# Attention with a top-32 search, a dense layer and a routed layer: which engine copies the last 64 keys of each tile into the search's tile

## The chip, the cores and the metric

The kernel runs on one core of a Trainium2 chip. The time is device time in microseconds (us) of one execution. Engines are called TensorE (PE; PEld is its weight load), VectorE (DVE), ScalarE (ACT), GpSimd (POOL) and SyncE (SP), as the profile's rows call them in brackets.

## What is computed

Three stages, one after the other, in float32:

```python
# q, k, v: (4, 8, 576, 64)
scores = np.matmul(q, k.transpose(0, 1, 3, 2)) / np.sqrt(64)
kth = np.partition(scores, -32, axis=-1)[..., -32:-31]
scores = np.where(scores >= kth, scores, -1e9)
attn = softmax(scores); x = attn @ v                 # then (2304, 512)
h = x @ w_in                                         # 512 -> 2048
x = (np.maximum(h, 0) + np.log1p(np.exp(-np.abs(h)))) @ w_out
# routed layer: 8 experts, each token goes to the argmax of x @ w_gate
out[mask] = gate[mask] * (np.maximum(x[mask] @ w1[e], 0) @ w2[e])
```

For every query row the 32nd largest of its 576 scores has to be found. That search is what the change touches.

## The kernel before

*Part one* computes attention and the dense layers, *part two* the routed layer. A tile is 128 query rows of one head; two tiles make a group, and there are 72 groups. Ten units of one or two finished row blocks go through the dense layers; a unit starts when the products of its last group are done. A unit has 16 steps: 12 matmuls into a bank (L646), two ScalarE functions (L660, L661) and the second layer's matmuls (L686).

For a group `emit_scores` has TensorE write the scores of the first 256 keys into bank `sa`, which ScalarE copies to the tile `s` (L466), and those of the other 320 keys into the tile `sb` in PSUM, one bank for each of its two tiles (L456). There is one buffer of `sa` and one of `sb`. `emit_softmax` then searches:

- L496 to L499 on VectorE take the larger of two keys, then of four, for the first 512 keys. L496 writes into a free part of `sb`, L497 into `s`, L498 and L499 into the tile `wk`: the larger halves in columns 0 to 127, the smaller in 128 to 255.
- L500 copies the last 64 keys of both tiles from `sb` into columns 256 to 319 of `wk`.
- L501 on VectorE writes the smaller ones of the first pairing into the last 256 columns of `wk`.
- L502 on ScalarE copies the 320 scores from `sb` to `s`. After it TensorE may write the next group's scores into `sb`.
- L506, L518 and L522 on VectorE find eight maxima at a time, four times, and strike them out between. The first two rounds look at 128 columns, the third at 320, the fourth at all 576.
- L529 on ScalarE scales the 32nd value; L530 (ScalarE), L531 (GpSimd), L532 (ScalarE, the exponential), L540 (ScalarE) and L541, L542 (GpSimd) make the weights, which a DMA transposes. The products with v (L559, L561) follow three groups later, and L583 to L586 on VectorE scale them.

In the first groups VectorE (L249, L252), ScalarE (L247, L251, L258, L259) and GpSimd also decode the dense layers' weights.

The program is written group by group, but the order on each engine is set by a scheduler, which sorts the instructions with priorities given in the code and a model of their times. A change of one instruction moves others. Engines run their own instructions in order and wait for each other by semaphores.

Of the kernel before, what the change touches and what calls it, by code (L numbers as in the profile page):

```python
# [13 lines left out]
AF = mybir.ActivationFunctionType  # L14
# [186 lines left out]
def part_one(tc, ctx, q, k, v, w_in, w_out, const, ident, before, ones, iota_e, reg_e, wg, ids,  # L201
             ohcum, done, early, table, rows, flags, sums, w_sums, e_sums, kths):
    nc = tc.nc
# [255 lines left out]
    PS, QS, US = 4 * D, 2 * D, D  # L459
# [14 lines left out]
    def emit_softmax(gi):  # L474
        group = groups[gi]
        n = range(2)
        s2, ps = sc_t.pop(gi)
        s = [s2[:, i] for i in n]
        sc = [pair[g[0]][4] for g in group]
        flb = 1 if flags is None else FLB  # L480
        if gi % flb == 0:
            tops[0] = sm.tile([128, 2 * flb, 32], F32, name="mx", bufs=2)
        mx = tops[0][:, 2 * (gi % flb):2 * (gi % flb) + 2]
        kth = mx[:, :, 31:32]
        e = [row.tile([128, S], F32, name="e", bufs=3) for _ in n]
        bt = sm.tile([128, 2, 1], F32, name="bias")
        if flags is None:
            src = list(s)
            wk = [row.tile([128, S], F32, name="wk") for _ in n]
        else:  # L490


            gl = ps[:, :, PS + US:PS + US + QS]
            gh = s2[:, :, PS:PS + QS]
            w2 = row.tile([128, 2, S], F32, name="wk", bufs=WKB)
            nc.vector.tensor_tensor(out=gl, in0=ps[:, :, :QS], in1=s2[:, :, :QS], op=ALU.max)  # L496
            nc.vector.tensor_tensor(out=gh, in0=ps[:, :, QS:PS], in1=s2[:, :, QS:PS], op=ALU.max)  # L497
            nc.vector.tensor_tensor(out=w2[:, :, :QS], in0=gl, in1=gh, op=ALU.max)  # L498
            nc.vector.tensor_tensor(out=w2[:, :, QS:PS], in0=gl, in1=gh, op=ALU.min)  # L499
            nc.vector.tensor_copy(w2[:, :, PS:PS + US], ps[:, :, PS:PS + US])  # L500
            nc.vector.tensor_tensor(out=w2[:, :, PS + US:], in0=ps[:, :, :PS], in1=s2[:, :, :PS], op=ALU.min)  # L501
            nc.scalar.activation(s2[:, :, PS:], ps[:, :, :PS + US], AF.Copy)  # L502
            src = [w2[:, i, :QS] for i in n]
            wide = (QS, QS, PS + US, S)
        for i in n:
            nc.vector.max(out=mx[:, i, 0:8], in_=src[i])  # L506
        if flags is not None:
            nc.scalar.activation(bt, mx[:, :, 0:1], AF.Copy, scale=-SCORE, bias=LN_ESC)
        else:
            for i in n:  # L510
                nc.vector.tensor_scalar(bt[:, i], mx[:, i, 0:1], sc[i][:, 4:5], LN_ESC, op0=ALU.mult, op1=ALU.add)
        if flags is None:
            for i in n:
                nc.scalar.activation(e[i], s[i], AF.Exp, bias=bt[:, i], scale=sc[i][:, 3:4])
        for j in range(3):
            for i in n:
                to = wk[i] if flags is None else src[i]
                nc.vector.match_replace(out=to, in_to_replace=mx[:, i, 8 * j:8 * j + 8], in_values=src[i],  # L518
                                        imm_value=NEG)
                src[i] = to if flags is None else w2[:, i, :wide[j + 1]]  # L520
            for i in n:
                nc.vector.max(out=mx[:, i, 8 * j + 8:8 * j + 16], in_=src[i])  # L522
        if flags is not None and gi % FLB == FLB - 1:
            g0 = 2 * (gi - FLB + 1)
            nc.vector.tensor_reduce(flags[:, g0:g0 + 2 * FLB], tops[0][:, :, 15:32:8], op=ALU.min, axis=AX.X)
        for i in n:
            if flags is not None:
                if i == 0:
                    nc.scalar.activation(kths[:, 2 * gi:2 * gi + 2], kth, AF.Copy, scale=K_UP)  # L529
                nc.scalar.activation(e[i], s[i], AF.Relu, bias=kths[:, 2 * gi + i], scale=-K_UP)  # L530
                nc.gpsimd.tensor_tensor(out=e[i], in0=s[i], in1=e[i], op=ALU.subtract)  # L531
                nc.scalar.activation(e[i], e[i], AF.Exp, bias=bt[:, i], scale=SCORE)  # L532
                continue
            mk = row.tile([128, S], F16, name="mk", bufs=1)
            nc.vector.tensor_scalar(mk, s[i], kth[:, i], None, op0=ALU.is_ge)
            nc.gpsimd.tensor_tensor(out=e[i], in0=e[i], in1=mk, op=ALU.mult)
        for i in n:

            p16 = row.tile([128, R, 2, D], F16, name="p16", bufs=PB if flags is not None else 2).rearrange("p r s d -> p (r s d)")
            nc.scalar.activation(p16[:, 0:S], e[i], AF.Copy)  # L540
            nc.gpsimd.tensor_tensor(out=p16[:, S:S + D], in0=e[i][:, S - D:], in1=p16[:, S - D:S], op=ALU.subtract)  # L541
            nc.gpsimd.tensor_tensor(out=p16[:, S + D:], in0=e[i][:, 0:S - D], in1=p16[:, 0:S - D], op=ALU.subtract)  # L542
            pT = row.tile([128, R, 128], F16, name="pT", bufs=2 * LAG)
            nc.sync.dma_start_transpose(out=pT, in_=p16)
            pt_t[group[i]] = pT
# [302 lines left out]
    for i in range(-1, n + LAG):  # L848
# [26 lines left out]
        if 0 <= i < n:  # L875
            with tc.high_priority(offset=AHEAD):
                emit_softmax(i)
            with tc.high_priority(offset=0):
                decode_some(DECR)
# [285 lines left out]
```

## Time and profile before

| what | us |
|---|---|
| median of 3 runs | 1054.38 (1048.77 to 1056.56) |
| profiled execution, its own time | 1059.72 |
| span of the profiled execution, first to last instruction | 1058.0 |
| search, first to last group's start (L496) | 19.0 to 689.6 |
| VectorE busy | 849.3 |
| ScalarE busy | 801.2 |
| TensorE busy | 885.0 |

The runs and the profiled execution are different executions, so that the trace's times are added against 1059.72. Busy time of an engine is the union of its instructions; neighbours overlap by some 0.1 us, so that the place of an instruction in a row is a little less than its length.

### The profile page before, as it was taken

What the parts mean: (1) busy time and instruction counts of PE and PEld (TensorE: products, weight loads), DVE (VectorE), ACT (ScalarE), POOL (GpSimd) and SP (SyncE); (2) the same over time, 40 slices, a digit from 0 to 9 for tenths busy, and PEclk for the clock granted to TensorE, in tenths of its full rate; (3) what the DMA queues carried; (4) which work ended last, traced back from release to release, by engine and by line L of the source; (5) the groups of instructions that cost most, each with busy time, mean ns of one, the idle gap of its engine ahead of it and who ended that gap; (6) DMA issues with size and microseconds to landing.
All of it is one profiled execution on the core that took longest, in us unless ns stands there. A gap on an engine that the chain in (4) does not pass through costs nothing.

```text
span 1058.0 us, 22206 instructions
## 1 busy us (share of the span) xinstructions
PE 885.0 (84%) x7146; PEld 655.0 (62%) x7146; DVE 849.3 (80%) x3021; ACT 801.2 (76%) x1866; POOL 604.0 (57%) x631
## 2 busy tenths in 40 slices
PE   1124359774998989998999999999999999999994
PEld 0013236443675656675666666676787989999993
DVE  4779999998997968996989999955356987777773
ACT  5878898988888979987998888863678555555552
POOL 3888898998767768876778777652001022111111
PEclk9986559876999989998999999999999999999998
DMA  7897799788799987669978855464301667666650
GB/s 188 193 205 189 180 192 193 179 168 172 114 131 164 138 152 129 117 80 150 152 131 120 99 90 95 72 86 131 102 12 31 170 220 243 242 212 230 237 202 23
DMA packets 295859, 156.97 MB, mean 148 GB/s; under 512 B 257524, under 2 KB 257652, under 8 KB 295732
## 3 DMA queue, kind: packets, MB, share of 16 engines
q1 hardware_dynamic: 292116, 145.73, 67.1%
q0 software_dynamic: 3616, 9.72, 2.6%
q8 instruction: 58, 0.95, 0.4%
q14 instruction: 69, 0.57, 0.2%
HBM read 77.89 MB, written 11.11 MB: 84 GB/s over the span
## 4 chain that ended last, share of the span: by engine, by line
PE 47%; DVE 13%; DMA 12%; ACT 9%; POOL 8%; issue 6%; SPq 4%; POOLq 0%; ACTq 0%; DVEq 0%
PE h L646 11%; PE h L996 9%; PE y L686 8%; PE y L1009 8%; PE y L683 3%; DVE mx L522 3%; DVE wk L518 3%; DMA xT<-xh 3%; POOL e L531 2%; POOL p L542 2%; DMA w<-in_moe_w_in_dram 2%; PE sb L456 2%; PE m L559 1%; ACT e L532 1%; PE sa L456 1%
## 5 line engine op out<-in xcount | busy, mean ns | idle before, releaser
L646 PE MATMUL h<-xT,w_in_s 128*128 128x256 f16 (+1 forms) x1920 | 228.7, 269 | 22.9 <-ACT sa L660 14.4
L686 PE MATMUL y<-w_out_s,g 128*128 128x512 f32 x480 | 229.0, 601 | 1.3 <-ACT g L661 1.2
L646 PEld LDWEIGHTS <-w_in_s 128*128 128x128 f16 x1920 | 174.9, 101 | 82.7 <-issue 52.7
L531 POOL TENSOR_TENSOR e<-s,e 128x576 f32<-128x576 f32 x144 | 204.0, 1432 | 17.7 <-ACT e L530 10.4
L522 DVE MAX8 mx<-wk 128x8 f32<-128x128 f32 (+2 forms) x432 | 200.9, 503 | 0.1
L542 POOL TENSOR_TENSOR p<-e,p 128x512 f16<-128x512 f32 x144 | 167.8, 1165 | 0.0
L456 PEld LDWEIGHTS <-q 128*128 128x128 f16 (+1 forms) x640 | 55.8, 108 | 175.4 <-issue 125.8
L518 DVE MATCH_REPLACE8 wk<-mx,wk 128x128 f32<-128x128 f32 (+1 forms) x432 | 145.1, 343 | 0.1
L686 PEld LDWEIGHTS y<-w_out_s,g 128*128 128x128 f32 x480 | 82.7, 192 | 64.0 <-issue 58.1
L976 POOL DMA_INDIRECT out_dram<-ot,idx x19 | 19.5, 1028 | 176.1 <-DVE ot L975 173.4
L532 ACT ACTIVATE e<-e,bias 128x576 f32<-128x576 f32 x144 | 110.4, 768 | 12.7 <-POOL e L531 12.2
L996 PEld LDWEIGHTS h<-xT,wf 128*128 128x128 f32 x864 | 111.8, 191 | 5.4 <-ACT wf L957 0.2
L996 PE MATMUL h<-xT,wf 128*128 128x256 f32 x864 | 113.9, 283 | 0.0
L456 PE MATMUL sa<-kt,q 128*128 128x256 f16 (+1 forms) x320 | 54.0, 302 | 71.0 <-DMA kt<-st 23.4
L1009 PE MATMUL y<-wf,hT 128*128 128x512 f32 x432 | 112.8, 398 | 0.0
L456 PE MATMUL sb<-kt,q 128*128 128x320 f16 (+1 forms) x320 | 62.7, 338 | 53.6 <-ACT s L502 53.5
L530 ACT ACTIVATE e<-s,kths 128x576 f32<-128x576 f32 x144 | 104.9, 767 | 0.8
L559 PEld LDWEIGHTS <-pT 128*128 128x128 f16 (+1 forms) x1440 | 86.8, 106 | 22.9 <-issue 19.8
L559 PE MATMUL m<-v,pT 128*128 128x65 f16 (+1 forms) x1440 | 93.9, 201 | 7.2 <-DVE xtail L586 4.3
L540 ACT ACTIVATE p<-e 128x576 f16<-128x576 f32 x144 | 97.4, 678 | 0.7
L541 POOL TENSOR_TENSOR p<-e,p 128x64 f16<-128x64 f32 x144 | 46.1, 320 | 70.4 <-ACT p L540 65.9
L1009 PEld LDWEIGHTS y<-wf,hT 128*128 128x128 f32 x432 | 76.7, 189 | 13.0
(235 smaller groups left out, 1791.1 us busy)
## 6 DMA issues: line engine op xcount, KB each, us to landing
w1r<-in_moe_w_dram SPq DMA_DIRECT2D x20, 1024.0 KB, 6.3
w2r<-in_moe_w_dram SPq DMA_DIRECT2D x20, 1024.0 KB, 7.8
w<-in_moe_w_in_dram SPq DMA_DIRECT2D x16, 512.0 KB, 4.0
w<-in_moe_w_out_dram SPq DMA_DIRECT2D x16, 512.0 KB, 4.0
rows<-xr SPq DMA_DIRECT2D x37, 128.2 KB, 3.1
qn<-in_q_dram SPq DMA_DIRECT2D x16, 288.0 KB, 4.1
kn<-in_k_dram SPq DMA_DIRECT2D x16, 288.0 KB, 6.1
vn<-in_v_dram SPq DMA_DIRECT2D x16, 288.0 KB, 3.5
```

The lines of the kernel that those rows point to most:

```text
L456: last_qk[0] = nc.tensor.matmul(ps[p0:p1], lhsT=qs[:, h, r0:r1, :].rearrange("p r d -> p (r d)"), rhs=kt[:, k0:k1, cs], start=first, stop= ...
L518: nc.vector.match_replace(out=to, in_to_replace=mx[:, i, 8 * j:8 * j + 8], in_values=src[i], imm_value=NEG)
L522: nc.vector.max(out=mx[:, i, 8 * j + 8:8 * j + 16], in_=src[i])
L530: nc.scalar.activation(e[i], s[i], AF.Relu, bias=kths[:, 2 * gi + i], scale=-K_UP)
L531: nc.gpsimd.tensor_tensor(out=e[i], in0=s[i], in1=e[i], op=ALU.subtract)
L532: nc.scalar.activation(e[i], e[i], AF.Exp, bias=bt[:, i], scale=SCORE)
L542: nc.gpsimd.tensor_tensor(out=p16[:, S + D:], in0=e[i][:, 0:S - D], in1=p16[:, 0:S - D], op=ALU.subtract)
L559: nc.tensor.matmul(o[:, h, 0:D + 1], lhsT=pT(r), rhs=v16[:, h, c, 0:D + 1], start=r == 0, stop=r == R - 1)
L646: nc.tensor.matmul(hps[:, :n], lhsT=w_in_s[:, c, j, p, o:o + 128], rhs=xT[:, 0:len(u.tiles), r, c, :], start=m == 0, stop=m == 3 * KD - 1)
L686: nc.tensor.matmul(u.y[i], lhsT=g[:, cs], rhs=w_out_s[:, f, :], start=f == 0, stop=f == KF - 1)
L996: nc.tensor.matmul(h, lhsT=w1f[:, a, c, :], rhs=xT[:, b, c, :], start=n == 0, stop=n == 3 * KD - 1)
L1009: nc.tensor.matmul(y[i], lhsT=hT[g][:, a, i * 128:i * 128 + 128], rhs=w2f[:, b, :], start=g == 0 and n == 0, stop=g == KF2 - 1 and n == 2)
```

## The change

The copy of the last 64 keys of both tiles (L500) is issued on ScalarE as an activation with the function Copy, in the place of VectorE's copy. Its operands are the same.

```diff
             nc.vector.tensor_tensor(out=w2[:, :, QS:PS], in0=gl, in1=gh, op=ALU.min)
-            nc.vector.tensor_copy(w2[:, :, PS:PS + US], ps[:, :, PS:PS + US])
+            nc.scalar.activation(w2[:, :, PS:PS + US], ps[:, :, PS:PS + US], AF.Copy)
             nc.vector.tensor_tensor(out=w2[:, :, PS + US:], in0=ps[:, :, :PS], in1=s2[:, :, :PS], op=ALU.min)
             nc.scalar.activation(s2[:, :, PS:], ps[:, :, :PS + US], AF.Copy)
```

The scheduler makes a new order of it on all engines. Two places show what it does around the copy, both in the group that begins at 306.57 us in the trace of before. What stands in brackets is the semaphore that an instruction waits for: DVE_49, Activation_49, PE_49 and Pool_49 are counted up by these engines, DMAHW by DMA queues.

VectorE from the group's last pairing (L499) on, before:

```order
L499 TENSOR_TENSOR wk<-sb,s 128x2x128
L500 COPY wk<-sb 128x2x64
L501 TENSOR_TENSOR wk<-sb,s 128x2x256
L506 MAX mx<-wk 128x8 [waits DVE_49]
L506 MAX mx<-wk 128x8
L586 TENSOR_TENSOR x_3135<-m,rc 128x128 [waits DVE_49]
L743 TENSOR_TENSOR h<-h,reg_e 128x8 [waits PE_49]
L518 MATCH_REPLACE wk<-mx,wk 128x128 [waits DVE_49] x2
L745 SCALAR_TENSOR_TENSOR ds,dst<-h,oh 128x8 [waits DVE_49]
L522 MAX mx<-wk 128x8 [waits DVE_49] x2
```

The same place after the change:

```order
L499 TENSOR_TENSOR wk<-sb,s 128x2x128
L506 MAX mx<-wk 128x8 [waits DVE_49]
L506 MAX mx<-wk 128x8
L586 TENSOR_TENSOR x_3135<-m,rc 128x128 [waits DVE_49]
L518 MATCH_REPLACE wk<-mx,wk 128x128 [waits DVE_49] x2
L501 TENSOR_TENSOR wk<-sb,s 128x2x256 [waits Activation_49]
L522 MAX mx<-wk 128x8 [waits DVE_49] x2
L518 MATCH_REPLACE wk<-mx,wk 128x128 [waits DVE_49] x2
```

The copy is gone, and L501, which had no wait, has moved behind the first round of the search and waits for ScalarE. The small instructions of the routing (L743, L745) stand elsewhere.

ScalarE in the same group, from the scaling of the 32nd value of the group before (L529) to the copy that frees `sb` (L502), before:

```order
L529 ACTIVATE kths<-mx 128x2 [waits DVE_49]
L530 ACTIVATE e<-s,kths 128x576 [waits Activation_49]
L530 ACTIVATE e<-s,kths 128x576 [waits Pool_49]
L417 ACTIVATE st,sums<-kn 128x9x64 [waits DMAHW0_49]
L502 ACTIVATE s<-sb 128x2x320 [waits DVE_49,PE_49]
```

After the change:

```order
L529 ACTIVATE kths<-mx 128x2 [waits DVE_49]
L530 ACTIVATE e<-s,kths 128x576 [waits Activation_49]
L530 ACTIVATE e<-s,kths 128x576 [waits Pool_49]
L532 ACTIVATE e<-e,bias 128x576 [waits Pool_49]
L540 ACTIVATE p_3920<-e 128x576 [waits DMAHW4_49,Activation_49]
L500 ACTIVATE wk<-sb 128x2x64 [waits DVE_49,PE_49]
L508 ACTIVATE bias<-mx 128x2 [waits DVE_49]
L532 ACTIVATE e<-e,bias 128x576 [waits Pool_49]
L466 ACTIVATE s<-sa 128x2x256 [waits PE_49]
L606 ACTIVATE xh<-x_3135 128x512 [waits DVE_49]
L660 ACTIVATE sa,e_sums<-h 128x256 [waits PE_49]
L417 ACTIVATE st,sums<-kn 128x9x64 [waits DMAHW2_49]
```

The new copy waits for VectorE (its L499) and stands behind two more instructions of the group before; L502 now comes after those shown, with one more L540 between.

## Rows read from the trace of the kernel before

**Rows 1.** The page: busy us, share of the span and instructions of each engine

```profile
PE 885.0 (84%) x7146; PEld 655.0 (62%) x7146; DVE 849.3 (80%) x3021; ACT 801.2 (76%) x1866; POOL 604.0 (57%) x631
```

**Rows 2.** By stretch: length, busy PE, PEld, DVE, ACT, POOL; clock, DMA share, GB/s

```profile
0.00:150.00 150.00, 43.21 (x385) 27.90 (x386) 120.35 (x397) 119.35 (x239) 116.44 (x126) 0.79 0.86 193
150.00:260.00 110.00, 81.52 (x664) 51.99 (x664) 102.42 (x332) 100.42 (x230) 101.21 (x99) 0.83 0.83 177
260.00:400.00 140.00, 128.64 (x1095) 86.79 (x1095) 118.05 (x492) 116.01 (x280) 103.75 (x111) 0.94 0.89 140
400.00:700.00 300.00, 290.16 (x2640) 197.29 (x2638) 278.68 (x1152) 262.58 (x644) 227.33 (x243) 0.99 0.73 110
700.00:1058.00 358.00, 341.44 (x2369) 291.05 (x2367) 229.78 (x652) 202.82 (x477) 55.27 (x56) 0.99 0.51 156
```

**Rows 3.** The chain that ended last: start us, length us, what

```profile
146.67 3.23 DMA xT<-xh
...
261.64 3.09 DMA xT<-xh
```

**Rows 4.** The timeline of VectorE over one group: start us, length us, instruction, idle before

```profile
306.57 0.42 DVE L496 TENSOR_TENSOR sb<-sb,s 128x256 f32<-128x256 f32 x1
...
308.29 0.28 DVE L500 COPY wk<-sb 128x128 f32<-128x128 f32 x1
308.49 0.68 DVE L501 TENSOR_TENSOR wk<-sb,s 128x512 f32<-128x512 f32 x1
309.09 0.48 DVE L506 MAX8 mx<-wk 128x8 f32<-128x128 f32 x2
...
310.07 0.28 DVE L518 MATCH_REPLACE8 wk<-mx,wk 128x128 f32<-128x128 f32 x1
...
313.17 1.41 DVE L522 MAX8 mx<-wk 128x8 f32<-128x576 f32 x2
314.75 0.43 DVE L496 TENSOR_TENSOR sb<-sb,s 128x256 f32<-128x256 f32 x1 [0.17 <-ACT s L466]
```

**Rows 5.** The timeline of ScalarE and TensorE over the same group

```profile
306.50 0.19 ACT L529 ACTIVATE kths<-mx 128x2 f32<-128x2 f32 x1
306.72 1.44 ACT L530 ACTIVATE e<-s,kths 128x576 f32<-128x576 f32 x2
...
310.37 0.69 ACT L502 ACTIVATE s<-sb 128x640 f32<-128x640 f32 x1
...
312.65 0.71 PE L456 MATMUL sb<-kt,q 128*128 128x320 f16 x4
```

**Rows 6.** Groups of instructions: busy us, mean ns of one, idle before

```profile
L532 ACT ACTIVATE e<-e,bias 128x576 f32<-128x576 f32 x144 | 110.4, 768 | 12.7 <-POOL e L531 12.2
L540 ACT ACTIVATE p<-e 128x576 f16<-128x576 f32 x144 | 97.4, 678 | 0.7
...
L466 ACT ACTIVATE s<-sa 128x512 f32<-128x512 f32 x72 | 42.0, 584 | 2.1 <-PE sa L456 2.0
...
L500 DVE COPY wk<-sb 128x128 f32<-128x128 f32 x72 | 20.2, 280 | 0.0
...
L508 ACT ACTIVATE bias<-mx 128x2 f32<-128x2 f32 x72 | 14.3, 199 | 0.0
```

**Rows 7.** What VectorE's L496 waited for: us in total, times

```profile
  ACT s L466: 30.4, 19
  PE sb L456: 10.5, 5
```

**Rows 8.** ScalarE's L502: what it waited for, then who waited for it

```profile
  DVE wk L501: 7.9, 13
...
  PE sb L456: 53.5, 18
```

**Rows 9.** The timeline of VectorE: the longest stop

```profile
497.78 0.43 DVE L496 TENSOR_TENSOR sb<-sb,s 128x256 f32<-128x256 f32 x1 [8.75 <-ACT s L466]
```

**Rows 10.** L496 alone by stretch: length, VectorE's busy us, count, clock, DMA share, GB/s

```profile
0.00:400.00 400.00, 16.05 (x38) 0.85 0.86 170
```

## The prediction

> **What bounds the kernel now.** I read first the page's busy times, then the table by stretch, the chain that ended last, one group of the search on VectorE and on ScalarE, the groups of instructions, and last who waits for the two instructions beside the copy.
>
> Over the whole span no engine is full: TensorE 84%, VectorE 80%, ScalarE 76% [rows 1]. By stretch it is otherwise [rows 2]. In the first 150 us TensorE works 43 us, while VectorE, ScalarE and GpSimd are busy 120, 119 and 116 us: three engines share the bound. From 150 to 260 us all three stand at 91 to 93%. From 400 us on TensorE is busy 290 of 300 us, then 341 of 358 us: the dense layers have a backlog there, and the search no longer sets the rate. Between, from 260 to 400 us, TensorE reaches 92%. The chain says the same in another way: it runs through the transposed rows that feed the first and the second unit of the dense layers, landing at 146.7 + 3.2 and 261.6 + 3.1 us [rows 3]. Until about 400 us the end is set by how fast groups are searched, and after it by TensorE. 38 of the 72 groups start before 400 us [rows 10]. What a group gains or loses there counts; what it gains later is hidden by TensorE.
>
> A group takes 8.18 us in the example (306.57 to 314.75), and VectorE works in it with hardly a pause: 0.17 us of idle time at its end, for ScalarE's copy of the next scores [rows 4]. TensorE writes the next group's second bank only at 312.65, long after ScalarE freed it at 310.37 + 0.69 [rows 5].
>
> **The change part by part.** *The copy leaves VectorE.* It lasts 0.28 us, 72 times, 20.2 us busy [rows 6]. But the instruction behind it starts 0.20 us after it (308.29, 308.49), since neighbours overlap [rows 4]: a place in the row costs 0.20 us, 14.4 us over 72. VectorE waited before L496 in 24 of 72 groups, 19 times for ScalarE's L466 and 5 for TensorE [rows 7], so in two thirds VectorE itself is the pace. In the first 38 groups that is 38 x 2/3 x 0.20 = **5.1 us gained**.
>
> *The copy joins ScalarE.* No row shows ScalarE moving 128 x 128 numbers out of a bank. From below it is bounded by L508 with 2 columns, 0.20 us, from above by L466 with 512 columns, 0.58 us [rows 6]; a straight line between them gives 0.29 us at 128 columns, an estimate. I take that, since both are plain ScalarE copies; 0.20 and 0.58 stay as ends. It counts where ScalarE was what came last, the 19 groups in 72 that waited for L466 [rows 7]: 38 x 0.26 x 0.29 = **2.9 us lost**, with ends 0 (the copy falls into ScalarE's pauses) and 38 x 0.29 = 11.0 us.
>
> *A new wait stands on VectorE's path.* L502 and L501 write different columns of different tiles, and share only the bank they read; yet ScalarE idled for L501 before L502 13 times, 7.9 us [rows 8]. So a bank is used by one engine at a time here, and in the new order L501 waits for ScalarE, which waits for L499. The Trainium skill has the rule behind this ("PSUM — Partial Sum Buffer", section on bank collisions): the compiler makes any two instructions of different engines on one bank and quadrant follow each other, reads too. By that rule the copy must stand between L499 and L501 on another engine's queue, and the trace agrees by the 7.9 us; if only what one writes and the other touches counted, the next term would be nothing and the sum would come out at about 1054.
>
> The scheduler covers most of the wait: L501 moves behind two L506 and often behind L518 and L522 as well. What is left is worked out per group by adding, from the rows' durations less the overlap, what stands on either engine. In the example ScalarE starts L529 at 306.50 and ends its two L530 at 306.72 + 1.44 = 308.16, 1.6 us after L496 [rows 5]. Now one L532 (0.77) and one L540 (0.68) [rows 6] stand next, each 0.1 less by overlap, then the copy: 1.6 + 0.67 + 0.58 + 0.29 = 3.1 us. VectorE comes to L501 after L499, two L506, L586 and two L518. From 309.09 these L506 to L518 ran until 310.07 + 0.28 = 310.35, 1.26 us, and start 0.80 us sooner without the copy and L501: at 309.55, 3.0 us after L496; without L743, which the new order has elsewhere, 2.8 us. VectorE stands 0.1 to 0.3 us. Done for groups 1 to 37, from the order and the same durations, 15 groups have ScalarE late, by 14.9 us in all; 12.2 of these lie in 9 groups before 260 us. There ScalarE begins its row sooner than assumed, because L496 itself waits for L466 [rows 7], so I count a third: 4.1 + 2.7 = **6.8 us lost**, with ends 0 and 14.9.
>
> *The bank comes free later.* L502 must follow L501, and now also stands behind the first L532 of the group before in 45 groups, where it did in 14. The same sums put its median end at 5.3 us after L496, where the example has 4.5 us (310.37 + 0.69 - 306.57) [rows 4, 5], 0.8 us more. TensorE waited for L502 18 times, 53.5 us [rows 8], but mostly early, when it has little to do; VectorE waited for the bank's scores in 5 groups only [rows 7]. The example shows why: scores at 312.65 leave 2 us to the next L496 [rows 4, 5]. So 38 x 5/72 x 0.8 = **2.1 us lost**; from below 0, from above, with every group TensorE waits in, 38 x 18/72 x 0.8 = 7.6 us.
>
> *What the cover hides.* L508 and L532 behind the copy on ScalarE feed the exponentials, which the products use three groups later; this cover goes only if ScalarE stops for a microsecond or more. The scores' layout, DMAs and their queues keep their instructions; SP and GpSimd are only reordered.
>
> The sum on the profiled execution: 1059.7 us (its span is 1058.0) - 5.1 + 2.9 + 6.8 + 2.1 = 1066.4 us, 0.63% more. The median of the runs is 1054.4, 0.5% under the profiled one, so the forecast is 1054.4 x 1.0063 = **1061.0 us**.
>
> **Rivals.** *Faster: VectorE is the pace and the rest hides.* For it: VectorE is busiest of all up to 400 us [rows 2], and all three costs are estimates with zero as one end. The gain is then 38 x 0.20 = 7.6 us. The new order also shuffles the long stops, of which one took 8.75 us while VectorE waited for L466 [rows 9]; losing one such stop gives 1054.4 - 7.6 - 8.75 = 1038 us. Against it: 24 groups waited for others [rows 7], and a new stop can appear as well as an old one vanish.
>
> *Slower: the bank's round trip becomes the pace.* L501, L502, the next scores, the next L496 form a ring over one buffer. In the example VectorE was through with the group at 313.17 + 1.41 = 314.58, 8.0 us after L496 [rows 4]; without the copy that is 7.8 us. TensorE, inside dense work, reached the scores 1.6 us after the bank was free and took 0.7 us for them [rows 5]. With L502 ending at 5.3 us that makes 5.3 + 1.6 + 0.7 = 7.6 us: 0.2 us are left. If TensorE comes later than that in most groups, every delay counts whole: 38 x 0.8 - 5.1 = 25.3 us, 1080 us. For it: the 53.5 us that TensorE stands for L502 already [rows 8]. Against it: the scheduler chose TensorE's order anew with the later release in view.
>
> *Nothing: TensorE hides it.* If its backlog begins sooner than 400 us, by its 92% between 260 and 400 us [rows 2], only the first 22 or so groups count, in which three engines share the bound, and gains and costs of 2 to 4 us cancel: 1054 us. Against it: the chain still passes through the search's own transfers there.
>
> **How the numbers follow.** What a measurement of this kernel can tell from no change is about 1%, 10.5 us: under 1043.8 is faster, over 1064.9 slower. The forecast has a chance of 0.48, with a range of its own from 1052 to 1072; 0.30 of it lies within 1%, 0.18 above. The faster rival has 0.24, the slower 0.15, nothing 0.13. That is 0.24 faster, 0.30 + 0.13 = 0.43 the same, 0.18 + 0.15 = 0.33 slower. With all costs at their upper ends the sum is 1054.4 - 5.1 + 11.0 + 14.9 + 7.6 = 1082.8; with none and a stop gone, 1038. The range is 1038 to 1083.
>
> **What would show it.** In the profile after, VectorE's copies are gone and its busy time is some 20 us less; ScalarE has 72 copies near 0.29 us. Before L501 VectorE idles for L500, in about a fifth of the groups, 5 to 15 us in all: near zero speaks for the faster rival. VectorE's wait for the scores of the second bank stays near 10 us; several times that speaks for the ring. The dense layers' second unit starts within a few us of 264.8. If VectorE's busy time falls and the second unit starts 5 us or more sooner, the step that let a third of the groups wait for others was wrong; if the search ends later and the whole does not, it was the step that put the boundary at 400 us.

## The result, and the profile after

The changed kernel takes 1064.09 us (median of 20 runs, 1058.84 to 1069.82) where the kernel before takes 1057.31 us beside it (20 runs). The ratio is 1.0063 with a 95% interval from 1.0047 to 1.0079. That is 0.6% slower, clear of no change, and less than the 1% named in the prediction. Its profiled execution took 1065.98 us with a span of 1063.9.

The page of the kernel after, busy us, share of the span and instructions of each engine:

```profile
PE 889.1 (84%) x7146; PEld 658.2 (62%) x7146; DVE 844.9 (79%) x2949; ACT 812.7 (76%) x1938; POOL 604.5 (57%) x631
```

Against [rows 1], 72 instructions have gone from VectorE to ScalarE. ScalarE is 11.5 us busier, VectorE only 4.4 us less busy: the lengths of all its instructions sum to 16.9 us less, but they also overlap by 12.5 us less, and busy time counts an overlap once.

By stretch, kernel after (length, busy PE, PEld, DVE, ACT, POOL; clock, DMA share, GB/s):

```profile
0.00:150.00 150.00, 45.99 (x392) 29.45 (x393) 119.39 (x392) 121.77 (x252) 117.91 (x127) 0.77 0.85 192
150.00:260.00 110.00, 80.93 (x647) 51.42 (x646) 97.43 (x300) 98.99 (x234) 97.08 (x95) 0.83 0.79 175
260.00:400.00 140.00, 127.66 (x1063) 86.33 (x1061) 110.94 (x458) 111.88 (x280) 97.59 (x104) 0.94 0.80 130
400.00:700.00 300.00, 285.50 (x2593) 194.15 (x2590) 265.97 (x1077) 262.62 (x668) 221.75 (x236) 0.98 0.65 112
700.00:1058.00 358.00, 349.06 (x2465) 296.83 (x2462) 251.13 (x728) 217.41 (x508) 70.16 (x72) 1.00 0.55 160
```

Beside [rows 2], VectorE is at work less in every stretch up to 700 us and 21 us more after it. TensorE has worked as long as before by 400 us (254.6 us, 253.4 before), although it has executed 42 matmuls fewer; from 400 to 700 us it does 4.7 us and 47 matmuls less. So about half of the matmuls by which it is behind at 700 us were lost where the prediction saw a backlog.

What came before and behind the two instructions that the change couples, kernel after. First who VectorE's L501 waited for, then who waited for it (us in total, times):

```profile
L501 DVE TENSOR_TENSOR wk<-sb,s x72: 666/680/693, 20.9 to 714.7; 128x512 f32<-128x512 f32 x72
...
  ACT wk L500: 20.5, 18
who waited for it (us, times):
  ACT s L502: 7.8, 8
```

The same view of the copy, ScalarE's L500 (durations in ns are minimum, median, maximum):

```profile
L500 ACT ACTIVATE wk<-sb x72: 250/263/293, 20.4 to 714.1; 128x128 f32<-128x128 f32 x72
...
  DVE wk L499: 5.2, 7
```

And what VectorE's first pairing L496 waited for:

```profile
L496 DVE TENSOR_TENSOR sb<-sb,s x72: 405/432/433, 18.7 to 712.2; 128x256 f32<-128x256 f32 x72
...
  PE sb L456: 20.5, 14
  ACT s L466: 19.3, 11
```

The new wait is there: VectorE stands 20.5 us in 18 groups before L501, which waited for nothing before. TensorE's scores come late in 14 groups instead of 5, for 20.5 us instead of 10.5; ScalarE's L466 is late less often, 19.3 us instead of 30.4 [rows 7]. The last group starts at 712.2 us, 22.6 us later than before, while the span grew by 5.9 us. (What TensorE stood for L502, 53.5 us in [rows 8], is now 85.5 us in 20 waits.)

The longest of the new waits shows where it comes from. VectorE's timeline, kernel after (start us, length us, instruction, idle before and who ended it):

```profile
390.99 0.41 DVE L499 TENSOR_TENSOR wk<-sb,s 128x256 f32<-128x256 f32 x1
...
397.64 0.69 DVE L501 TENSOR_TENSOR wk<-sb,s 128x512 f32<-128x512 f32 x1 [4.43 <-ACT wk L500]
```

ScalarE's timeline in the same group:

```profile
391.69 0.19 ACT L660 ACTIVATION_READ_ACCUMULATOR sa<-h 128x1 f32 x1
396.01 0.68 ACT L417 ACTIVATE st<-kn 128x576 f16<-128x576 f32 x1 [4.12 <-DMA kt<-st]
396.60 0.19 ACT L417 ACTIVATION_READ_ACCUMULATOR st<-kn 128x1 f32 x1
396.69 0.76 ACT L530 ACTIVATE e<-s,kths 128x576 f32<-128x576 f32 x1
397.35 0.26 ACT L500 ACTIVATE wk<-sb 128x128 f32<-128x128 f32 x1
```

L499 was done at 391.40. The copy could have run then; it stood in ScalarE's row behind an L417 whose buffer a DMA had still to read, and behind the L530 after it. VectorE inherited that stop, which it did not touch before. Over all 18 waits ScalarE itself was idle for 2.9 of the 20.5 us, nearly all of it in this one stop. Else it was busy with the copy itself (4.4 us) and with what stands before the copy in its row, 8.4 us of that with L530.

### The profile page after: what moved, and what is told of

It reads as the page before. It is cut to its first block, busy times and chain, and to the rows that moved or that the text cites. A ratio compares the mean times of both kernels' runs of the same rounds, so it can differ in the third digit from the quotient of the medians.

```text
span 1063.9 us, 22251 instructions
## 1 busy us (share of the span) xinstructions
PE 889.1 (84%) x7146; PEld 658.2 (62%) x7146; DVE 844.9 (79%) x2949; ACT 812.7 (76%) x1938; POOL 604.5 (57%) x631
## 4 chain that ended last, share of the span: by engine, by line
PE 45%; DVE 14%; DMA 14%; ACT 9%; POOL 7%; issue 5%; SPq 4%; POOLq 0%; DVEq 0%; ACTq 0%
PE h L996 10%; PE y L1009 9%; PE h L646 9%; PE y L686 6%; DVE mx L522 4%; DVE wk L518 3%; PE y L683 3%; DMA xT<-xh 3%; DMA kt<-st 3%; POOL e L531 2%; POOL p L542 2%; DMA pT<-p 2%; PE sb L456 1%; PE m L559 1%; ACT e L532 1%
## 5 line engine op out<-in xcount | busy, mean ns | idle before, releaser
L646 PE MATMUL h<-xT,w_in_s 128*128 128x256 f16 (+1 forms) x1920 | 226.6, 268 | 13.6 <-ACT w_in_s L259 8.0
L686 PE MATMUL y<-w_out_s,g 128*128 128x512 f32 x480 | 231.6, 603 | 4.9 <-ACT g L661 4.8
L646 PEld LDWEIGHTS <-w_in_s 128*128 128x128 f16 x1920 | 174.2, 101 | 77.1 <-issue 41.2
L522 DVE MAX8 mx<-wk 128x8 f32<-128x128 f32 (+2 forms) x432 | 201.1, 502 | 0.1
L518 DVE MATCH_REPLACE8 wk<-mx,wk 128x128 f32<-128x128 f32 (+1 forms) x432 | 145.1, 342 | 0.1
L456 PE MATMUL sb<-kt,q 128*128 128x320 f16 (+1 forms) x320 | 63.7, 342 | 85.5 <-ACT s L502 85.5
L686 PEld LDWEIGHTS y<-w_out_s,g 128*128 128x128 f32 x480 | 82.5, 193 | 63.4 <-issue 54.7
L530 ACT ACTIVATE e<-s,kths 128x576 f32<-128x576 f32 x144 | 105.1, 767 | 1.3 <-POOL p L542 0.4
L559 PEld LDWEIGHTS <-pT 128*128 128x128 f16 (+1 forms) x1440 | 89.9, 108 | 19.9 <-issue 15.9
L559 PE MATMUL m<-v,pT 128*128 128x65 f16 (+1 forms) x1440 | 97.1, 204 | 3.7 <-DVE xtail L586 2.3
L540 ACT ACTIVATE p<-e 128x576 f16<-128x576 f32 x144 | 97.6, 680 | 2.5 <-DMA pT<-p 2.1
L456 PE MATMUL sa<-kt,q 128*128 128x256 f16 (+1 forms) x320 | 53.9, 307 | 46.1 <-DMA kt<-st 22.6
```

Source lines behind the costliest of these rows:

```text
L456: last_qk[0] = nc.tensor.matmul(ps[p0:p1], lhsT=qs[:, h, r0:r1, :].rearrange("p r d -> p (r d)"), rhs=kt[:, k0:k1, cs], start=first, stop= ...
L559: nc.tensor.matmul(o[:, h, 0:D + 1], lhsT=pT(r), rhs=v16[:, h, c, 0:D + 1], start=r == 0, stop=r == R - 1)
L646: nc.tensor.matmul(hps[:, :n], lhsT=w_in_s[:, c, j, p, o:o + 128], rhs=xT[:, 0:len(u.tiles), r, c, :], start=m == 0, stop=m == 3 * KD - 1)
L686: nc.tensor.matmul(u.y[i], lhsT=g[:, cs], rhs=w_out_s[:, f, :], start=f == 0, stop=f == KF - 1)
```

## The experiments

All are compared with the kernel before on the same chip, with six or twelve runs of each. Three theories stood first: *the handed-over bank costs* (a copy on ScalarE between two readers of `sb` makes VectorE wait and the bank come free later), *ScalarE's work costs* (its extra instructions alone), and *the order costs* (the scheduler lays out all engines anew, and the new layout is worse whatever the copy does).

### The copy behind the minima, and the copy from SBUF

```diff
-            nc.vector.tensor_copy(w2[:, :, PS:PS + US], ps[:, :, PS:PS + US])
             nc.vector.tensor_tensor(out=w2[:, :, PS + US:], in0=ps[:, :, :PS], in1=s2[:, :, :PS], op=ALU.min)
+            nc.scalar.activation(w2[:, :, PS:PS + US], ps[:, :, PS:PS + US], AF.Copy)
             nc.scalar.activation(s2[:, :, PS:], ps[:, :, :PS + US], AF.Copy)
```

> ScalarE's copy of the last 64 keys stands in the program behind VectorE's last pairing (the minima), so that the bank goes from VectorE to ScalarE once and does not come back. Theory (the return of the bank costs: VectorE's wait for the copy, 20.5 us in 18 groups of the changed kernel, and the late release of the bank): no wait of VectorE for the copy before the minima is left, VectorE's waits for the bank's scores fall back to some 10 us, and the time is at or under that of before, ratio 0.992 to 1.002. Rival A (ScalarE's own extra 72 x 0.26 us is what costs): the time stays where the changed kernel is, ratio 1.004 to 1.008. Rival B (the new order of the scheduler costs, whatever the reason): anything within 1%, with no tie to those waits.

Measured: 1.0198 (1.0165 to 1.0232). In the other one the copy no longer reads the bank:

```diff
-            nc.vector.tensor_copy(w2[:, :, PS:PS + US], ps[:, :, PS:PS + US])
             nc.vector.tensor_tensor(out=w2[:, :, PS + US:], in0=ps[:, :, :PS], in1=s2[:, :, :PS], op=ALU.min)
             nc.scalar.activation(s2[:, :, PS:], ps[:, :, :PS + US], AF.Copy)
+            nc.scalar.activation(w2[:, :, PS:PS + US], s2[:, :, 2 * PS:], AF.Copy)
```

> ScalarE takes the last 64 keys not from the bank but from the scores' tile in SBUF, after its own copy of the 320 scores. ScalarE has the same 72 extra instructions, VectorE the same one less, and the bank is released as early as before. Theory (the bank's return costs): ratio 0.990 to 1.001, with VectorE's wait before the minima gone; a wait before the third search round may appear, under 5 us. Rival A (ScalarE's extra work costs): ratio 1.004 to 1.008, as in the changed kernel. Rival B (order alone): anything within 1%.

Measured: 1.0207 (1.0169 to 1.0245). Two rows of the list of waits, first of the copy behind the minima (engine, line, waited for: us in total, times, longest):

```profile
DVE mx L522 <- ACT wk L501: 17.0, 14, 4.8
```

then of the copy from SBUF:

```profile
DVE mx L522 <- ACT wk L502: 39.9, 24, 5.5
```

In neither does VectorE wait before the minima any more, and both are 2% slower, more than the change. The wait has only moved, to the third round, which is the next reader of the copied keys. So the simple form of the first theory falls: without a visit to the bank between VectorE's reads the time is no better. Any copy on ScalarE makes VectorE depend on ScalarE's row. But each of these kernels also has an order of its own, so neither is a clean measure.

### ScalarE's visit to the bank by itself, between and behind

The kernel before, with a small read of the bank by ScalarE added. Its result goes to `junk`, a small tile of its own that nobody reads. The read stands once between VectorE's copy and the minima, and once behind the minima. (The line that makes `junk` is left out here.)

```diff
             nc.vector.tensor_copy(w2[:, :, PS:PS + US], ps[:, :, PS:PS + US])
+            nc.scalar.activation(junk, ps[:, :, PS:PS + 32], AF.Copy)
             nc.vector.tensor_tensor(out=w2[:, :, PS + US:], in0=ps[:, :, :PS], in1=s2[:, :, :PS], op=ALU.min)
```

> VectorE keeps its copy; ScalarE reads 2 x 32 of the bank's last keys into a tile that nobody uses, at the place where the changed kernel's copy stands, between the last maxima and the minima. Only the visit to the bank is added, no work is taken from VectorE. Theory (the return of the bank costs): VectorE waits for ScalarE before the minima, some 15 to 25 us in all, and the time is up by more than in the changed kernel, ratio 1.006 to 1.015. Rival A (ScalarE's work costs): as much as the next run, which has the same work in another place. Rival B (order alone): anything within 1%.

> The same extra read by ScalarE as in the run before, but behind the minima, so that the bank does not go back to VectorE. Theory (the return of the bank costs): VectorE waits for nothing before the minima; ScalarE's 72 x 0.24 us and a release of the bank that much later cost 0 to 5 us, ratio 1.000 to 1.005, clearly under the run before. Rival A (ScalarE's work costs): the same ratio as the run before, within 0.3%. Rival B (order alone): anything within 1%.

Measured: between 1.0325 (1.0287 to 1.0362), behind 1.0076 (1.0048 to 1.0105). The waits between:

```profile
DVE sb L497 <- PE sb L457: 35.4, 16, 6.0
...
DVE wk L503 <- ACT junk L502: 14.5, 10, 4.9
```

and behind:

```profile
DVE sb L497 <- PE sb L457: 11.6, 6, 5.9
```

(Lines stand one lower here: L497 is the first pairing; in the run between, L502 is the added read and L503 the minima.) A read that writes nothing the minima touch, and shares only the bank with them, still holds them up, 14.5 us in 10 groups. That is the rule of the Trainium skill ("PSUM — Partial Sum Buffer", section on bank collisions), that instructions of two engines on one bank and quadrant are put one behind the other, reads too; the trace agrees by those 14.5 us. (The prediction read the rule off L501 and L502, which share more than the bank: both use the tile `s` too, in different columns. This run has no such overlap.) The same work costs 2.5% more between than behind. How much of that is the two waits, and how much the two different orders, these runs don't tell.

### More work on either engine, in a free order

```diff
             nc.vector.tensor_copy(w2[:, :, PS:PS + US], ps[:, :, PS:PS + US])
+            nc.vector.tensor_copy(w2[:, :, PS:PS + US], ps[:, :, PS:PS + US])
```

> VectorE makes its copy twice, ScalarE none: only the price of 72 more places in VectorE's row. Forecast's step (a place is 0.20 us and counts in two thirds of the first 38 groups, 5.1 us): ratio 1.002 to 1.008. If VectorE's places cost nothing, 1.000 within 0.2%; if the search's whole slowdown reached the end, 72 x 0.20 = 14 us, 1.014.

Measured: 1.0122 (1.0087 to 1.0158), more than the forecast's step gives. And on ScalarE, behind L502, on SBUF, result unused:

```diff
             nc.scalar.activation(s2[:, :, PS:], ps[:, :, :PS + US], AF.Copy)
+            nc.scalar.activation(junk, s2[:, :, 2 * PS:2 * PS + 32], AF.Copy)
```

> VectorE keeps its copy; ScalarE makes an extra copy of 2 x 32 numbers from the scores' tile in SBUF, behind its copy of the 320 scores, into a tile that nobody reads: ScalarE's extra work alone, with no visit to the bank and nobody waiting for it. Theory now (an engine that waits for a copy in ScalarE's late queue costs most; the extra work little): ratio 1.000 to 1.005, below the late visit to the bank (1.0076). Rival A (the extra work itself is what costs): 1.006 to 1.010, as the late visit. Rival B (order alone): no forecast within 1%.

Measured: 1.0183 (1.0144 to 1.0221). Taken by itself this says that 18 us of work on ScalarE, for which nothing waits, cost 19 us of time. The runs with the order held, further down, show that it doesn't.

### A new order and nothing else

One priority of the scheduler changed by 1%, no instruction added, removed or changed.

```diff
-A_SC = 100
+A_SC = 101
```

> The kernel before with one of the scheduler's priorities, that of the scores, at 101 in the place of 100: the same instructions in another order on all engines. It measures rival B, what a new order does by itself. Theory: within 0.5% of before, ratio 0.995 to 1.005. Rival B: a move of 0.6% or more either way, so that the changed kernel's 0.63% says nothing of the copy.

Measured: 1.0045 (1.0022 to 1.0068). The same with the other priority:

```diff
-AHEAD = 100
+AHEAD = 101
```

> The kernel before with the priority of the search at 101 in the place of 100: a second sample of what a new order does by itself. Theory: ratio 0.995 to 1.005. Rival B: a move of 0.6% or more either way.

Measured: 1.0114 (1.0080 to 1.0149). The same instructions in another order cost 0.7 times and 1.8 times what the whole change costs. A result of this size can't be put down to the edited instruction before its order is held.

### The orders held

In the last four kernels the order of every engine is written down (`want` in the code), and held by dependences between neighbours in the row that need no semaphore:

```diff
+def hold_order(tc, nc, extra):
...
+    for engine, row in want.items():
+        last = None
+        for n in row:
+            i = traced[n]
...
+                if last is not None:
+                    tc.add_manual_dep(i, last.name, mybir.DependencyInfo(
+                        mybir.DependencyClass.NoSync, mybir.DependencyReason.DATA), reason="held order")
+                last = i
```

In their traces every engine's row is, instruction by instruction, that of the kernel whose order is held, but for the instructions named below. A kernel with a held order and no other edit was not run. For the old order the last run below, 0.39% with work added, leaves little for the holding itself; for the new order nothing bounds it.

One has the order of the kernel after, with VectorE's copy put back right ahead of L501:

```diff
-            nc.scalar.activation(w2[:, :, PS:PS + US], ps[:, :, PS:PS + US], AF.Copy)
+            nc.vector.tensor_copy(w2[:, :, PS:PS + US], ps[:, :, PS:PS + US])
```

The other has the order of the kernel before with ScalarE's copy (the change's own diff). The copy stands there behind both L530 of the group before, and L501 behind two L506 and two L518, as in 49 of 72 groups of the new order, if not further back; all else, L502 too, is where it was.

> The order of the changed kernel is held on all engines, and only the copy goes back to VectorE, right ahead of the minima; ScalarE has none. So the waits for the copy are gone and the order stays. Theory (the copy's way over ScalarE is what costs 0.63%): the time falls by some 0.5 to 1% against the changed kernel, ratio to before 0.996 to 1.003. Rival B (the new order costs, the copy's move by itself gains or does nothing): ratio 1.005 to 1.012, at the changed kernel or above it.

> The order of the kernel before is held on all engines. Only the copy moves: to ScalarE, behind both L530 of the group before, and VectorE's minima go behind two L506 and two L518, as in most groups of the changed kernel. Theory (the copy on ScalarE costs, by waits for it and a later release of the bank): VectorE waits for it 5 to 20 us, ratio 1.002 to 1.010. Rival B (only the new order costs): VectorE's 72 places are saved at no cost, ratio 0.993 to 1.001.

Measured: the new order with VectorE's copy 1.0155 (1.0124 to 1.0185); the old order with ScalarE's copy 1.0147 (1.0115 to 1.0180). Both are slower than any range that was expected of them. With the two kernels of the case that makes four corners:

| ratio to the kernel before | copy on VectorE | copy on ScalarE |
|---|---|---|
| order of the kernel before | 1 | 1.0147 |
| order of the kernel after | 1.0155 | 1.0063 |

Read along the rows: in the old order the move costs 1.5%, in the new order it gains 0.9% (1.0063 / 1.0155). Read down the columns: the new order costs 1.5% with the copy on VectorE and gives back 0.8% with it on ScalarE. Each order does better with the copy it was made for. "The move costs so much, the order so much" has therefore no single answer; what can be said is that the move into the old order, at these places, costs 1.5%, and that the scheduler's new order wins back over half of it.

The places matter. They were set by hand, and L502 kept its own although L501 moved back. What ScalarE waited for before L502 in that run:

```profile
  DVE wk L501: 32.2, 48
```

That was 7.9 us in 13 groups in the kernel before [rows 8] and 7.8 us in 8 in the kernel after. How much of the 1.5% comes from it was not tested.

What VectorE waited for before L501, old order and copy on ScalarE (us in total, times):

```profile
  ACT wk L500: 32.3, 26
```

In the kernel after it is 20.5 us in 18 groups. The new order does hide more of the wait. In 33 groups it has L501 behind two L522 as well, where the held old order has none; that this is the reason is argued, not tested. A price of the order shows in the run in which VectorE copies in the new order. There is no wait before L501 there, yet its L496 waits like this:

```profile
  PE sb L456: 24.6, 16
  ACT s L466: 19.3, 9
```

That is more for `sb` than in the kernel after (20.5), and much more than the 10.5 us of [rows 7]; TensorE stood 86.0 us for L502, as in the kernel after (85.5). Counted in the timelines, L502 ends 5.8 us after its group's L496 here (median), 5.9 us in the kernel after and 4.5 us in the kernel before. The bank's later release belongs to the new order, not to the engine that copies.

The waits also suggest why the same move gains in one order and costs in the other. All waits of VectorE before L496 sum to 60.3 us in this run and to 44.9 us in the kernel after. So 15.4 of the 20.5 us before L501 stand in the place of waits that were there anyway, and the 5.1 us left are less than the 14.4 us of 72 places in VectorE's row. In the old order the waits before L496 fall from 41.8 to 35.6 us only: 26.1 of the 32.3 us are new, more than 14.4 us. The differences, 9.3 us gained and 11.7 us lost, are near the 0.9% and 1.5% measured (some 10 and 16 us). This is a sum from one execution of each kernel, not a test.

The other two hold the old order and add the two loads of before (the same two diffs), each right behind its neighbour in the row:

> The order of the kernel before is held; VectorE makes its copy twice. The price of 72 places of VectorE without a new order. Forecast's step: 5.1 us, ratio 1.003 to 1.007. All 14.4 us would be 1.014; nothing, 1.000.

> The order of the kernel before is held; ScalarE makes an extra copy of 2 x 32 numbers in SBUF behind each L502, into a tile that nobody reads. ScalarE's extra work without a new order. Forecast's step (2.9 us of 72 x 0.26): ratio 1.000 to 1.005. Rival A (the work itself costs): 1.006 or more. The 1.0183 of the same extra copy under a new order was then the order's if this stays under 1.005.

Measured: VectorE's copy twice 1.0119 (1.0083 to 1.0155), the extra work on ScalarE 1.0039 (1.0017 to 1.0062). So of the 1.83% above, only 0.39% was ScalarE's work; 1.4% came with the order. VectorE's 1.2% is the same in both. The place of the second copy, from VectorE's timeline at the held order:

```profile
311.34 0.61 DVE L500 COPY wk<-sb 128x128 f32<-128x128 f32 x2
311.87 0.68 DVE L501 TENSOR_TENSOR wk<-sb,s 128x512 f32<-128x512 f32 x1
```

L501 starts 0.53 us after the first copy, where one copy took 0.20 [rows 4]: 0.33 us for the second, 23.8 us over 72. The time grew by 0.0119 x 1061.5 = 12.6 us (1061.5 us is the kernel before in these runs): 53% of VectorE's added time arrives at the end (37 to 69% by the interval). On ScalarE 72 x 0.256 = 18.4 us were added and 0.0039 x 1061.5 = 4.1 us arrived, 22% (10 to 36%).

By stretch, VectorE's copy twice at the held order (columns as before):

```profile
260.00:400.00 140.00, 125.47 (x1061) 84.75 (x1061) 121.15 (x507) 113.85 (x273) 100.76 (x107) 0.92 0.89 138
400.00:700.00 300.00, 284.01 (x2588) 193.93 (x2586) 279.86 (x1151) 258.91 (x632) 225.01 (x239) 0.99 0.69 110
```

TensorE works 3.2 us less than before from 260 to 400 us and 6.2 us less from 400 to 700 us [rows 2]: a slower VectorE is felt on TensorE after 400 us too.

No kernel tried was faster than the one before.

## Why the prediction was right or wrong

The forecast was 1061.0 us or 0.63% more, and 0.63% more was measured. The direction is right, and the wait that it named is there: VectorE stands before L501, because the bank has two readers and ScalarE's row is late. That this wait is what makes the kernel slower is not shown. In the old order the move costs 1.5%. But the kernel after has the new order: with that held the move gains 0.9%, and what costs 1.5% there, with VectorE's copy, is the order, which no term held. So the agreement of the two figures is luck: most terms were too small, in both directions, and the order's own cost is in the total. The terms in turn:

**VectorE's copy, 5.1 us gained.** Somewhat undersized. If a copy taken away gives back what a copy added costs, with 53% of a place arriving, it is 72 x 0.20 x 0.53 = 7.6 us, an estimate (5.3 to 9.9 by the interval). The two steps "in two thirds VectorE itself is the pace" and "only the first 38 groups" together let 35% arrive (38/72 x 2/3); for the doubled copy they give 38 x 2/3 x 0.33 = 8.4 us, just under the interval of the 12.6 measured (8.8 to 16.5).

**The boundary at 400 us.** This is the step that failed: what a group loses after 400 us is not hidden by TensorE. The chain that ended last had hinted at it in the kernel before. The prediction quoted its first two transposes and left out the later ones, and the stretch between the last two, in which the chain runs along VectorE's search, group by group:

```profile
483.90 9.18 DMA xT<-xh
...
639.97 4.42 DMA xT<-xh
...
665.80 0.45 DVE sb L496
...
681.72 0.44 DVE sb L496
...
708.04 6.93 DMA xT<-xh
```

The runs agree. The 38th group's L496 in VectorE's timeline, kernel before:

```profile
399.75 0.43 DVE L496 TENSOR_TENSOR sb<-sb,s 128x256 f32<-128x256 f32 x1
```

VectorE's copy twice at the held order:

```profile
404.14 0.43 DVE L496 TENSOR_TENSOR sb<-sb,s 128x256 f32<-128x256 f32 x1 [0.38 <-ACT s L466]
```

ScalarE's copy at the held order:

```profile
407.65 0.43 DVE L496 TENSOR_TENSOR sb<-sb,s 128x256 f32<-128x256 f32 x1 [0.38 <-ACT s L466]
```

So the two are 4.4 and 7.9 us late at 400 us. The last group starts 11.2 us late with VectorE's copy twice (700.8) and the span grows by 13.4; it starts 15.2 us late with ScalarE's copy (704.8) and the span grows by 15.3. The 6.8 and 7.3 us lost after 400 us arrived with the rest; nothing of the delay was hidden. TensorE's 290 busy us of 300 [rows 2] were no reserve. The same row has its weight loads at work in 197 of the 300 us, and in 291 of 358 us after 700 us; why TensorE doesn't catch up, no run shows.

The test that the prediction set for this step, a search that ends later while the whole does not, did come out in the kernel after, 22.6 us against 5.9, but for another reason. Dense matmuls of the first layer (L646) up to the last group's start, before:

```profile
0.00:690.00 690.00, 172.40 (x1380) 0.91 0.81 146
```

and after:

```profile
0.00:712.00 712.00, 176.36 (x1429) 0.91 0.74 141
```

In the new order some 50 more of them, and 17 of the second layer (L686), stand ahead of the last group. At 0.12 and 0.48 us of TensorE's time each (busy time of the line by its count) that is, as an estimate, about 14 of the 22.6 us: work done sooner, not work lost.

**ScalarE's copy, 2.9 us lost.** About right. A copy takes 0.263 us (0.29 estimated), and with 22% arriving 72 x 0.266 x 0.22 = 4.2 us, an estimate. In the old order ScalarE's work itself is the smaller part, 0.39% where the whole move costs 1.47%. In the new order no run has it alone.

**The wait before L501, 6.8 us.** Seen, and where it was to be expected. Counted in the timeline, VectorE stood 3.8 us in 3 groups before 260 us (4.1 was kept there after discounting), 8.1 us in 4 groups from there to 400 us (2.7 forecast, and 4.4 of the 8.1 is the one stop behind a DMA shown above), and 8.6 us in 11 groups after 400 us, which the prediction didn't count.

**The late release, 2.1 us.** The sign is right, the size is not known. VectorE waited for the bank's scores 20.5 us in 14 groups, twice the 10.5 us of before and not the "several times" of the ring. The release itself is later than forecast, 5.9 us after L496 where 5.3 was said. But it is as late with VectorE's copy in the same order, so it came with the order. No run isolates its price: what is left for the wait, the release and the order together is 6.7 (0.0063 x 1057.3) + 7.6 - 4.2 = 10.1 us where the prediction had 6.8 + 2.1 = 8.9; in the old order the same remainder is 15.6 + 7.6 - 4.2 = 19.0 us.

**What would show it.** "VectorE's busy time some 20 us less" was wrong by the prediction's own reckoning of 14.4 us for 72 places, and 4.4 us came. The copies at 0.263 us, the idle time before L501 in a quarter of the groups (a fifth was said), and the second unit at 263.4 us (264.8) are as described; 20.5 us of idle time are more than the 5 to 15.

**The rivals.** *Faster* falls: it had the waits near zero. The gain it builds on is real, but only within an order that has already paid. *The ring* falls as the pace: 25 us did not come, and the bank's waits only doubled. *Nothing, since TensorE hides it*, falls too: the slowdown is clear of no change, and in the held order TensorE hid none of the delay. The rival that was missing is the order. One mechanism should have held a chance of its own: the scheduler lays the program out anew, and two such layouts of the unchanged kernel came out 0.5% and 1.1% slower.

What stays open: why the scheduler's other orders are worse than the one of the kernel before (only two neighbours of it were tried), what of the 1.5% in the old order is due to the places chosen by hand, and why TensorE, busy some 95% or more from 400 to 700 us, passes the search's delays on.

## What to carry to other kernels

Where a scheduler lays out the program, hold its order before putting a result of a per cent down to the edited instruction, and measure what a neighbouring order of the unchanged kernel costs: here an extra load read 1.8% in a free order and 0.4% in a held one. A copy given to another engine makes its reader depend on that engine's row: ask what stands ahead of it there and how long that can stop, not only how long the copy takes. And follow the chain that ended last to its end before drawing a line behind which work is called hidden: here delays of a stage ahead came through whole, although TensorE was busy some 95% of the time or more.

## What the runs showed that was not expected

A change of one scheduling priority from 100 to 101 moves the time by 0.5% and 1.1%, with the same instructions. A read of a bank by ScalarE whose result nobody uses makes the kernel 3.3% slower between two of VectorE's reads and 0.8% slower behind them, each in an order of its own, with waits of VectorE for TensorE's next scores of 35.4 and 11.6 us. And 72 copies of 128 x 128 numbers leaving VectorE lower its busy time by 4.4 us, not by the 20.2 us that they lasted (by 12.2 us with the old order held).
